# Linear attention and a mixture of four experts: batch 0's attention in head pairs and token halves, and a written order for every engine up to tile 1

## The chip, the core and the metric

The kernel runs on one core of one Trainium2 chip. The time is in device microseconds (us) of that core, the median of several executions. Engines: TensorE (PE: products; PEld: its weight loads), VectorE (DVE), ScalarE (ACT), GpSimd (POOL) and SyncE (SP), and 16 DMA engines. DMAs are asked for by SP, ACT or POOL; POOL's can change the type on the way.

## What is computed

```python
# q, k, v: (8, 8, 576, 64) float32; w1: (4, 512, 1024); w2: (4, 1024, 512); domain_probs: (4608, 4)
def attn(q, k, v):
    phi = lambda x: np.where(x > 0, x, np.exp(x) - 1.0) + 1.0
    q_p, k_p = phi(q), phi(k)
    kv = np.einsum('bhsd,bhse->bhde', k_p, v)
    num = np.einsum('bhsd,bhde->bhse', q_p, kv)
    den = np.einsum('bhsd,bhd->bhs', q_p, k_p.sum(axis=2))[..., None] + 1e-06
    return num / den

x = attn(q, k, v).transpose(0, 2, 1, 3).reshape(4608, 512)
p = domain_probs / (domain_probs.sum(-1, keepdims=True) + 1e-09)
out = sum(p[:, e:e+1] * (np.maximum(x @ w1[e], 0) @ w2[e]) for e in range(4))
```

phi(x) is min(exp(x), max(x + 1, 1)), and that is how the kernel makes it.

## The kernel before

Tokens go in nine tiles of 512. Tile j < 8 is batch j's tokens 0 to 511; tile 8 is the eight leftovers of 64 tokens. All weights stay in SBUF in float16. For a tile, each expert runs layer 1 (512 to 1024, then ReLU) and layer 2 (1024 to 512, added into `acc` with the token's share `p`). Tile 0 runs expert 0's layer 1 plainly (`layer1_group`, L552: eight groups of four 128x512 products) and its layer 2 plainly for all experts (`layer2_part`, L607). Everything else is Strassen-like with seven products for eight: layer 1 in `Block` (`p1` to `p7`, L761), layer 2 in `layer2_product` (L696), with sums of weights on DVE (`weight_sums`, `weight_sums2`), of tokens (`token_sum`) and of hidden rows (`hidden_sum`, POOL, L663 to L669).

Attention of a batch: raw q, k, v arrive in four pieces each of two heads and 512 tokens (four tokens a partition, 1 KB runs), and the 64 leftover tokens apart (`rl`). `phi_act` takes exp on ACT, `phi_dve` the rest on DVE; `vcast` (L339) casts v and leaves room for a column of ones, which gives the denominator; `kv` (L444, and L436 or L452 for the leftovers) makes the 64x65 sums of a pair of heads, and copies its two diagonal blocks into `kvz`, zero elsewhere (L468); `pe_qT` turns q (L423); `nd` (L492) makes numerators and denominators, 128x130 a product; `norm` (L474, L475) takes the reciprocal and multiplies; `pe_xT` (L529, copy L531) turns x so that layer 1 can read it. A leftover x is turned at L414.

Order: every engine runs its instructions in the order in which the program emits them. For batch 0 that order is `CFG["START"]`, a list of steps in which a number n means n filler products (`warm`, L888) on a tile of zeros. All later work is put at positions (`put_at`, from `CFG["ATTN"]`, `L2P`, `BLK` and so on), sorted, and emitted whole: a step's products and the copies behind them come together.

DMA: batch 0's raw tiles are asked for by SP and ACT (L277, L255; `CFG["B0"]`), the weights and batch 1's raw tiles by POOL (`load_first`; L185 for w1 of expert 0 in quarters, L188 for other w1, L182 for w2; order `CFG["DMA"]`), later batches by SP. PSUM has eight banks as four tags of two buffers: `s`, `e`, `b`, `py`; attention's tiles take their tag in turn (`aps`).

Of the kernel before, what the change touches and what calls it, by code (L numbers as in the profile page):

```python
# [1 line left out]

# [18 lines left out]
    "DMA": ('w100', 'w101', 'w102', 'w103', 'k0', 'w201', 'lk1', 'w200', 'w111', 'w110', 'w121', 'w120', 'lv0', 'lk0', 'w211', 'w210', 'v2', 'v1', 'v0', 'k1', 'w130', 'lv1', 'w131', 'q0', 'k2', 'k3', 'v3', 'w220', 'q2', 'q1', 'w221', 'q3', 'w230', 'w231'),  # L21
# [51 lines left out]
    "MODE": {'k0': 0, 'q2': 1, 'k3': 0, 'q0': 0, 'k2': 0, 'k1': 1, 'q1': 0, 'q3': 0, 'T3': 0, 'T0': 0, 'T1': 1, 'v1': 2, 'v2': 0, 'v3': 2, 'v0': 0, 'T2': 1},  # L73
    "APS": ('s', 'e', 'b', 'py'),
    "START": (11, 'qa1', 'qa0', 'ka0', 'qd1', 'lv', 'qd0', 2, 'qT1', 'kd0', 5, 'qT0', 'ka1', 'v1', 'lka', 'lkd', 'v0', 7, 'kv0', 'qa2', 'kd1', 'ka2', 'qa3', 3, 'nd0', 'kd2', 7, 'kv1', 'qd2', 'v2', 'qd3', 'dma0', 'v3', 4, 'nd1', 'qT2', 1, 'kv2', 'ka3', 3, 'xT0', 'dma1', 'kd3', 'qT3', 'nd2', 'xT1', 1, 'kv3', 'ph1', 1, 'nd3', 'ph2', 'xT2', 'xT3', 1, 'ph0'),
    "B0": ('slk', 'aq0', 'slv', 'aq1', 'sv0', 'sv1', 'sq2', 'sk2', 'ak0', 'sq3', 'sv2', 'sv3', 'ak1', 'sk3'),
    "CAST": (),
}
# [3 lines left out]
def kernel(  # L82
# [11 lines left out]
    CAST = CFG["CAST"]  # L94
    ATTN, HSUM, L2ORD, L2AT, MODE = (CFG[x] for x in ("ATTN", "HSUM", "L2ORD", "L2AT", "MODE"))
# [32 lines left out]
    make_identity(nc, identh)  # L128

# [14 lines left out]
    w1_sb = [pw.tile([P, DC, F], FP16, tag=f"w1_{e}", name=f"w1_{e}") for e in range(E)]  # L144
    w2_sb = [pw.tile([P, FC, Dm], FP16, tag=f"w2_{e}", name=f"w2_{e}") for e in range(E)]
# [5 lines left out]
    s1_sb = [pw.tile([P, 3, 2, F // 2], FP16, tag=f"s1_{e}", name=f"s1_{e}") for e in range(E)]  # L151


    t2_sb = {e: pw.tile([P, 3, FH, DH], FP16, tag=f"t2_{e}", name=f"t2_{e}") for e in SE}
# [9 lines left out]
    turn = {"aps": ["s", "e"], "ph": ["b", "py"]}  # L164

    def bank(kind, shape, dtype, name):
        tag = turn[kind][0]
        turn[kind] = turn[kind][1:] + [tag]
        return ppm.tile(shape, dtype, tag=tag, bufs=2, name=name)

    def aps(shape, dtype, name):
        return bank("aps", shape, dtype, name)

# [4 lines left out]
    def load_w(layer, e, r):  # L178

        if layer == 2:  # L180
            fs = slice(r * 4, r * 4 + 4)
            nc.gpsimd.dma_start(out=w2_sb[e][:, fs], in_=w2_src[e, :, fs])  # L182
        elif e == 0:
            fs = slice(r * F // 4, (r + 1) * F // 4)
            nc.gpsimd.dma_start(out=w1_sb[e][:, :, fs], in_=w1_src[e, :, :, fs])  # L185
        else:
            ds = slice(r * 2, r * 2 + 2)
            nc.gpsimd.dma_start(out=w1_sb[e][:, ds], in_=w1_src[e, :, ds])  # L188

    def load_first(lo, hi):  # L190

        parts = [x for x in CFG["DMA"] if x[0] in "kq"]
        homes = dict(zip(parts, [None] * NRAW + ["acc", None]))
        homes.update(v0="hs1", v1="hs1", v2="hs3", v3="hs3")
        if lo > 0:
            b1.alloc_left()
        for x in CFG["DMA"][lo:hi]:
            if x[0] == "w":
                load_w(*map(int, x[1:]))
            elif x[0] == "l":  # L200
                b1.load_left(x[1], eng=nc.gpsimd, us=(int(x[2]),))
            else:
                b1.load(x[0], int(x[1]), nc.gpsimd, home=homes[x])

    def load_probs(eng, first):
# [12 lines left out]
        raws.append(t)  # L218

    def emit_probs(first):  # L220
        t = raws.pop()[:, 0:1] if first else raws.pop()[:, 1:NTILES]
# [14 lines left out]
    raws = []  # L236
# [3 lines left out]
    class Batch:  # L240
        def __init__(self, b):
            self.b = b
            self.raw, self.ph, self.pairs = {}, {}, {}
            self.kvz, self.kl, self.qTl = kvzs[min(b, 1)], kz, qz
            self.ps = b >= 1
# [4 lines left out]
        def load_left(self, *names, eng=nc.sync, us=(0, 1)):  # L250
            b = self.b
            for i, (name, src) in enumerate((("k", k), ("v", v), ("q", q))):
# [9 lines left out]
        def load(self, name, i, eng=nc.sync, home=None):  # L262
# [3 lines left out]
            if home is None:  # L266
                t = praw.tile(shape, FP16 if self.b == 1 and name in CAST else FP32, tag="raw", name="rawb")
# [14 lines left out]
        def alloc(self):  # L282
            self.kp = pa.tile([P, CM, H, D], FP16, tag="kp", bufs=1, name="kp")
            if self.b == 1:
                self.vp = bts[0].vp
            else:
                self.vp = pa.tile([P, CM, H, DE], FP16, tag="vp", bufs=1, name="vp")
                nc.gpsimd.memset(self.vp[:, :, :, D:DE], 1.0 / SX)
            self.vl = vl
            if self.b < 1:  # L290
                self.qp = pm.tile([P, CM, H, D], FP16, tag="h", bufs=NHB, name="qp")
            if self.b < 1:
                self.diag = pa.tile([P, 2, DE], FP16, tag="xsl", bufs=1, name="diag")
                nc.gpsimd.memset(self.diag, 0.0)
                for u in range(2):
                    nc.gpsimd.memset(self.diag[u * HP : (u + 1) * HP, u], 1.0)
            self.qT = pa.tile([P, CM, NPAIR, P], FP16, tag="qT", bufs=1, name="qT")
            if self.b < 1:
                self.x = pm.tile([P, NPAIR, CM, P], FP16, tag="tt", bufs=2, name="x_sb")
            if self.b < 1:  # L300
                self.new_xT()
# [4 lines left out]
        def phi(self, name, i):  # L306
            self.phi_act(name, i)
            self.phi_dve(name, i)

        def phi_act(self, name, i):  # L310

            if self.b >= 1 and (name, i) == ("q", 0):
# [3 lines left out]
            if self.ps or MODE.get(f"{name}{i}") == 1:  # L316
                nc.scalar.activation(dst.rearrange("p c h d -> p h c d"), src, AF.Identity, bias=1.0)
                ee = aps([P, HQ * CM * D], FP32, "psum_ee")
            else:
                ee = pm.tile([P, HQ * CM * D], FP16, tag="hs0", bufs=2, name="ee")  # L320
            ee = ee.rearrange("p (c h d) -> p c h d", c=CM, h=HQ)
            nc.scalar.activation(ee.rearrange("p c h d -> p h c d"), src, AF.Exp)
            self.ph[name, i] = src, dst, ee

        def phi_dve(self, name, i):
            src, dst, ee = self.ph.pop((name, i))
            dst, ee = (a.rearrange("p c h d -> p c (h d)") for a in (dst, ee))
            if self.ps or MODE.get(f"{name}{i}") == 1:
                nc.vector.scalar_tensor_tensor(
                    out=dst, in0=dst, scalar=1.0, in1=ee, op0=AO.max, op1=AO.min  # L330
                )
            else:
                hd = dst.rearrange("p c (h d) -> p h c d", h=HQ)
                (nc.gpsimd if MODE.get(f"{name}{i}") == 2 else nc.vector).tensor_scalar(hd, src, 1.0, 1.0, AO.add, AO.max)
                nc.vector.tensor_tensor(out=dst, in0=ee, in1=dst, op=AO.min)

        def vcast(self, i):
            eng = nc.gpsimd if self.b == 0 and MODE.get(f"v{i}") == 2 else nc.scalar
            (eng.copy if eng is nc.scalar else eng.tensor_copy)(  # L339
# [4 lines left out]
        def left_act(self, *names):  # L344

            for name in names:
# [3 lines left out]
                if name == "k" and self.b < 1:  # L350
                    self.kn = pa.tile([P, HG, D], FP16, tag="qlp", bufs=1, name="kn")
                    parts.append((slice(0, P), self.kn.rearrange("p h d -> p (h d)")))
                for u in range(2) if name == "k" and self.b >= 1 else ():
# [5 lines left out]
                if self.ps:  # L359
                    for us, dst in parts:  # L360
                        nc.scalar.activation(dst, src[us], AF.Identity, bias=1.0)
                    el = aps([P, HG * D], FP32, "psum_el")
                else:
                    el = pm.tile([P, HG * D], FP16, tag="hs0", bufs=2, name="el")
                nc.scalar.activation(el, src, AF.Exp)
                self.ph["l" + name] = src, el, parts

        def left_v(self, eng=nc.scalar):
            (eng.copy if eng is nc.scalar else eng.tensor_copy)(
                out=self.vl[:, :, 0:D], in_=self.rl[:, 1]  # L370
            )

        def left_dve(self, name):
            src, el, parts = self.ph.pop("l" + name)
            for us, dst in parts:
                if self.ps:
                    nc.vector.scalar_tensor_tensor(
                        out=dst, in0=dst, scalar=1.0, in1=el[us], op0=AO.max, op1=AO.min
                    )
                else:  # L380
                    nc.vector.tensor_scalar(dst, src[us], 1.0, 1.0, AO.add, AO.max)
                    nc.vector.tensor_tensor(out=dst, in0=el[us], in1=dst, op=AO.min)

        def left_kv(self):
            self.left_act("k")
            self.left_dve("k")
            self.left_v(nc.gpsimd)

        def dma_qT(self):
# [671 lines left out]
```

## Time and profile before

| | |
|---|---|
| median of 3 runs | 496.31 us (495.79 to 496.56) |
| the profiled execution's span | 494.1 us |
| HBM read, written | 45.16 MB, 9.44 MB |
| DMA, mean over the span | 109 GB/s |
| PE fillers (L888) | 46 products of 128x512 |

The profile's page gives busy time by engine, the span in 40 slices, the DMA queues, the chain that ended last and the costliest groups. The trace behind it can be asked for busy time by stretch, a timeline by engine, and who waited for whom. Products are pipelined and their ends are modelled, so a product's price is better read from the start of one to the start of the next than from its mean duration. POOL's DMA rows give bytes as written (float16); twice as many are read where float32 weights are cast.

### The profile page before, as it was taken

The page shows a single profiled execution, that of the slowest core. Times are in us where ns is not written, and L with a number is a line of the kernel's source. Part 1 is how long each engine was busy: PE and PEld are TensorE (multiplying, and loading weights), DVE is VectorE, ACT ScalarE, POOL GpSimd, SP SyncE. Part 2 cuts the span into 40 slices and gives each one's busy share as a digit, 9 for nine tenths or more (in the row PEclk, how much of TensorE's full clock was granted, in tenths as well). Part 3 has the DMA queues.
Part 4 walks back from the last instruction along what each step waited for, and adds up shares of the span by engine and source line. Part 5 has one row for each costly group of instructions (what it writes and reads, how often), then busy time and mean ns, then how long its engine had stood idle before and what let it go on. Part 6 is the DMA issues. An engine that isn't in the chain of part 4 may idle for free.

```text
span 494.1 us, 11611 instructions
## 1 busy us (share of the span) xinstructions
PE 483.7 (98%) x4346; PEld 409.3 (83%) x4346; DVE 379.5 (77%) x800; ACT 336.7 (68%) x678; POOL 357.0 (72%) x344
## 2 busy tenths in 40 slices
PE   9999999999999999999999999999999999999996
PEld 3557656878898989898989898989898888888885
DVE  5639988799867987698859886888687756775686
ACT  6768969954988488848894789468954565446530
POOL 3735204878977797769776977698669877987775
PEclk9999999999999999999999999999999999999999
DMA  8999966542465234533464255523231020002003
GB/s 261 222 214 247 262 134 189 161 106 49 110 188 116 55 111 161 132 69 93 134 165 82 71 150 139 102 53 94 87 74 35 4 96 1 1 1 87 1 1 86
DMA packets 82104, 53.65 MB, mean 109 GB/s; under 512 B 46240, under 2 KB 75808, under 8 KB 82048
## 3 DMA queue, kind: packets, MB, share of 16 engines
q1 hardware_dynamic: 70512, 40.00, 31.0%
q0 software_dynamic: 9888, 11.41, 12.2%
q10 hardware_dynamic: 1648, 1.51, 1.1%
q8 instruction: 34, 0.56, 0.5%
q14 instruction: 22, 0.18, 0.1%
HBM read 45.16 MB, written 9.44 MB: 111 GB/s over the span
## 4 chain that ended last, share of the span: by engine, by line
PE 79%; DMA 11%; DVE 5%; ACT 3%; POOL 1%; issue 1%; SPq 0%; ACTq 0%; DVEq 0%
PE py L696 37%; PE pb L761 21%; PE pe L761 16%; DMA w<-in_moe_w_dram 9%; DVE acc L598 2%; PE py L607 1%; DMA rawb<-in_v_dram 1%; DVE x_sb L475 1%; PE psum_nd L492 1%; PE psum_kv L444 1%; DVE h L745 1%; POOL w L185 1%; DMA rawh<-in_q_dram 1%; PE pb L696 1%; ACT u L772 0%
## 5 line engine op out<-in xcount | busy, mean ns | idle before, releaser
L598 DVE SCALAR_TENSOR_TENSOR acc<-py,p_sb,acc 128x256 f32<-128x256 f32 (+1 forms) x382 | 182.4, 488 | 44.3 <-PE py L696 39.6
L745 DVE CUSTOM_DVE_ANT_0 h<-pe,u 128x512 f16<-128x512 f32 x140 | 96.4, 688 | 44.1 <-PE pe L761 26.1
L761 PEld LDWEIGHTS <-w 128*128 128x128 f16 x1120 | 108.9, 98 | 17.3 <-issue 1.2
L663 POOL TENSOR_TENSOR hs<-h 128x512 f16<-128x512 f16 x64 | 74.2, 1159 | 54.4 <-DVE h L745 53.3
L696 PEld LDWEIGHTS <-h 128*128 128x128 f16 x1024 | 99.6, 98 | 12.3 <-issue 0.9
L696 PE MATMUL py<-w,h 128*128 128x256 f16 x744 | 106.4, 273 | 0.0
L772 ACT COPY u<-pb 128x512 f32<-128x512 f32 x140 | 83.0, 593 | 27.4 <-PE pb L761 25.5
L665 POOL TENSOR_TENSOR hs<-hs,h 128x512 f16<-128x512 f16 x64 | 74.3, 1160 | 27.5 <-PE py L696 24.9
L761 PEld LDWEIGHTS <-s 128*128 128x128 f16 x840 | 81.6, 98 | 11.9
L761 PE MATMUL pb<-tt,w 128*128 128x256 f16 x560 | 84.0, 273 | 0.1
L696 PEld LDWEIGHTS <-hs 128*128 128x128 f16 x768 | 74.4, 98 | 8.8 <-issue 0.4
L669 POOL TENSOR_TENSOR hs<-h,hs 128x512 f16<-128x512 f16 x64 | 75.3, 1177 | 3.6 <-PE py L696 3.2
L696 PE MATMUL py<-t,hs 128*128 128x256 f16 x496 | 74.4, 273 | 0.1
L667 POOL TENSOR_TENSOR h<-h 128x512 f16<-128x512 f16 x64 | 74.3, 1162 | 0.0
L787 ACT ACTIVATE h<-pe 128x512 f16<-128x512 f32 x70 | 42.0, 600 | 45.0 <-PE pe L761 44.2
L781 ACT COPY pe<-pb 128x512 f32<-128x512 f32 x70 | 40.1, 573 | 41.6 <-PE pb L761 15.4
L805 ACT ACTIVATE h<-pb 128x512 f16<-128x512 f32 x70 | 42.1, 601 | 9.6 <-PE pb L761 9.5
L761 PE MATMUL pe<-tt,s 128*128 128x256 f16 x280 | 42.0, 273 | 0.0
L761 PE MATMUL pb<-tt,s 128*128 128x256 f16 x280 | 42.0, 273 | 0.0
L761 PE MATMUL pb<-xT,w 128*128 128x256 f16 x248 | 37.2, 273 | 0.4 <-DMA w<-in_moe_w_dram 0.4
L761 PE MATMUL pe<-xT,w 128*128 128x256 f16 x248 | 37.2, 273 | 0.3 <-ACT pe L781 0.3
L761 PE MATMUL pe<-xT,s 128*128 128x256 f16 x248 | 37.2, 273 | 0.0
(125 smaller groups left out, 609.6 us busy)
## 6 DMA issues: line engine op xcount, KB each, us to landing
out_dram<-acc SPq DMA_DIRECT2D x32, 256.0 KB, 2.5
w<-in_moe_w_dram POOLq DMA_DIRECT2D x14, 512.0 KB, 12.2
rawb<-in_v_dram SPq DMA_DIRECT2D x26, 256.0 KB, 2.8
rawb<-in_q_dram SPq DMA_DIRECT2D x26, 256.0 KB, 2.8
rawb<-in_k_dram SPq DMA_DIRECT2D x26, 256.0 KB, 3.2
w<-in_moe_w_dram POOLq DMA_DIRECT2D x4, 256.0 KB, 5.7
rawb<-in_k_dram POOLq DMA_DIRECT2D x4, 256.0 KB, 8.0
rl<-in_q_dram SPq DMA_DIRECT2D x16, 64.0 KB, 2.7
```

What stands on the lines that cost most here:

```text
L598: nc.vector.scalar_tensor_tensor(out=acc, in0=ps, scalar=pscal, in1=acc, op0=AO.mult, op1=AO.add)
L663: nc.gpsimd.tensor_tensor(out=hs[0], in0=a21, in1=a22, op=AO.add)
L665: nc.gpsimd.tensor_tensor(out=hs[1], in0=hs[0], in1=a11, op=AO.subtract)
L667: nc.gpsimd.tensor_tensor(out=a21, in0=a11, in1=a21, op=AO.subtract)
L669: nc.gpsimd.tensor_tensor(out=hs[3], in0=a12, in1=hs[1], op=AO.subtract)
L696: nc.tensor.matmul(out=ps, lhsT=lhsT(k), rhs=rhs[:, k], start=first and k == 0, stop=k == FH - 1, skip_group_check=True,)
L745: nc.vector._custom_dve(TENSOR_ADD_SAT, out=out, in0=ps, in1=u, s0=BIG, s1=0.0)
L761: nc.tensor.matmul(out=ps[:, kk], lhsT=lk(kc), rhs=rhs[:, kc], start=first and kk == 0 and kc == 0, stop=kc == 1, skip_group_check=True,)
L772: nc.scalar.copy(u, self.b)
L781: nc.scalar.copy(self.e5, self.b)
L787: nc.scalar.activation(self.h[:, :, 0, 0:NH], self.e5, AF.Relu)
L805: nc.scalar.activation(self.h[:, :, 1, 0:NH], self.b, AF.Relu)
```

## The change

Batch 0 gets a class of its own (`First`). Its k and v come as pairs of heads, all 576 tokens, nine tokens a partition (64 partitions a head), so that batch 0 has no leftover k and v apart. Its q comes in four pieces: a half of the tokens (two of four a partition) of four heads. The sums of k and v are 18 products of 64x65 for a pair, one head into PSUM partitions 0 to 63 and the other into 64 to 127. q and x are turned by halves of the tokens; numerators of two pairs go into one PSUM tile and their denominators into another, with one reciprocal and one multiplication for both. Layer 1 of expert 0 in tile 0 runs by halves of the tokens, two groups of 128 hidden rows together (`layer1_half`). Tiles for raw k and v and their results use the space of weights that come later (`s1`, `t2`, `w1`, `w2` of experts 2 and 3). ACT no longer asks for DMAs at the start. Batches 1 to 7 keep their attention, but batch 1's numerators are emitted in two halves, and phi has one form (`phi_act`, `phi_dve` with exp in PSUM).

Most functions become generators: a `yield` parts the products from the copies behind them. `CFG["EARLY"]` names, in order, which function goes on next, from the first load up to tile 2's first blocks; it replaces `START`, `B0`, `MODE` and `APS`. Names: `lq`, `lk`, `lv` loads; `ke`, `kl`, `km` exp, add-and-max, min of k; `qe`, `ql`, `qm` the same of q; `vc` cast of v; `qT`, `xT` transposes; `nd` numerators; `Lgh` layer 1 of row group g and half h; `p1.010` product 1 of tile 0, expert 1, half 0; `y0.12` layer 2 of expert 0, rows 1, part 2; `s`, `t` weight sums; `m` layer 2 products; `b1.` batch 1. What is left after the list is emitted in the order before. `CFG["BANK"]` names the PSUM tag of a step.

```diff
+    "CUT": (((0, 3, 4), (0, 3, 4), (0, 4), (0, 4)), ((0, 2, 4),) * 4),
+    "WARM": (14, 5, 3, 1, 2, 1, 1),
-    "START": (11, 'qa1', 'qa0', 'ka0', 'qd1', 'lv', 'qd0', 2, 'qT1', 'kd0', 5, 'qT0', 'ka1', 'v1', 'lka', 'lkd', 'v0', 7, 'kv0', 'qa2', 'kd1', 'ka2', 'qa3', 3, 'nd0', 'kd2', 7, 'kv1', 'qd2', 'v2', 'qd3', 'dma0', 'v3', 4, 'nd1', 'qT2', 1, 'kv2', 'ka3', 3, 'xT0', 'dma1', 'kd3', 'qT3', 'nd2', 'xT1', 1, 'kv3', 'ph1', 1, 'nd3', 'ph2', 'xT2', 'xT3', 1, 'ph0'),
-    "B0": ('slk', 'aq0', 'slv', 'aq1', 'sv0', 'sv1', 'sq2', 'sk2', 'ak0', 'sq3', 'sv2', 'sv3', 'ak1', 'sk3'),
+    "EARLY": (
+        "lq0 lk3 lk1 ql0 qe0 lq2 ke1 ql2 kl1 w103 qe2 ke3 kl3 lv1 w100 lk0 lq1 km1 qm0 ke0 kl0 w102 w101 km3 warm0 qT0 ql1 lv0 qm2 km0 vc1 vc0 w111 lq3 ql3 qT0",
+        "warm1 kv1 kv1 lk2 qe3 lv2 vc2 kv1 qT2 qT2 lv3 rk1 kv0 w110 ke2 qe1 kv0 kv0 qm3 vc3 kl2 warm2 nd01 nd00 warm3 qT3 v0 nd00 w200 nd01 warm4 xT10 kv3 xT11",
+        "km2 kv2 kv2 qT3 xT11 xT10 kv2 xT01 kv3 w201 kv3 qm1 xT01 warm5 qT1 rk0 xT00 nd11 qT1 xT00 L01 rv1 nd10 nd11 warm6 xT31 nd10 rv0 L21 w120 xT21 L11 xT31",
+        "L31 xT21 L31 lpr0 L01 L31 xT20 xT20 k3 xT30 L11 w121 L01 v2 xT30 s0.0 L21 v1 L30 L11 L30 L20 L10 L21 p1.010 ts0.0 L20 p1.010 L00 ts0.2 b1.v0 L10 ts0.1",
...
+        "s2.0 s2.1 s2.3 b1.v1 p2.021 y0.13 p2.020 p6.020 p6.021 p6.020 t0.3 s2.2 y0.23 p6.021 b1.km3 p5.020 p7.020 b1.v2 q2 y0.23 s0.2 y1.10 t1.0 p7.020",
+        "c22.020 b1.k1 p5.021 y1.11 p7.021 p7.021 w131 b1.km1 b1.k0 p4.020 p3.020 y1.20 y1.21 q0 b1.k2 p4.020 p4.021 c22.021 p3.020 b1.load5 p3.021 b1.km0",
+        "y1.12 b1.v3 p4.021 b1.kv0 b1.km2 b1.load0 b1.kv0 y1.13 b1.kv1 b1.kv1 p3.021 y1.22 y1.23 b1.q3 y1.30 y1.13 y1.23 q1 y1.31 y1.32 y1.33 b1.q2 p1.031",
...
+    kraw = [pw.tile([P, 2, TK, D], FP32, tag=f"{x}_{E - 1}", name=f"kraw{x}") for x in ("s1", "t2")]
+    vraw = [pw.tile([P, 2, TK, D], FP32, tag=f"{x}_{E - 2}", name=f"vraw{x}") for x in ("s1", "t2")]
+    kpos = pw.tile([P, NPAIR, TK, D], FP16, tag=f"w1_{E - 1}", name="kpos")
+    kexp = pw.tile([P, NPAIR, TK, D], FP16, tag=f"w2_{E - 1}", name="kexp")
+    vpos = pw.tile([P, NPAIR, TK, DE], FP16, tag=f"w2_{E - 2}", name="vpos")
...
+    class First(Batch):
...
+        def load_kv(self, name, i, eng):
+            t, src = {"k": (kraw, k), "v": (vraw, v)}[name]
+            eng.dma_start(
+                out=t[i // 2][:, i % 2].rearrange("p t d -> p (t d)"),
+                in_=src[0, 2 * i : 2 * i + 2].rearrange("h (p t) d -> (h p) (t d)", t=TK),
+            )
...
+        def q_lin(self, i, eng):
+            eng.tensor_scalar(self.q_part(i), self.raw["q", i], 1.0, 1.0, AO.add, AO.max)
...
+        def kv(self, i, engs):
+            ps = aps([P, DE], FP32, "psum_kv")
+            for t in range(TK):
+                for u in range(2):
+                    us = slice(u * HP, (u + 1) * HP)
+                    nc.tensor.matmul(
+                        out=ps[us],
+                        lhsT=kpos[us, i, t],
+                        rhs=vpos[us, i, t],
+                        start=t == 0,
+                        stop=t == TK - 1,
+                        skip_group_check=True,
+                    )
+            for u in range(2):
+                yield
+                us = slice(u * HP, (u + 1) * HP)
+                (engs[u].copy if engs[u] is nc.scalar else engs[u].tensor_copy)(
+                    out=self.kvz[us, i, u], in_=ps[us]
+                )
+
+        def x_norm(self, g, hf):
+            num = aps([P, 2, 2, 2, D], FP32, "psum_num")
+            den = aps([P, 2, 2, 2], FP32, "psum_den", "+")
+            for a in range(2):
+                for c in range(2):
+                    pair, lhsT = 2 * g + a, self.qT[:, 2 * hf + c, 2 * g + a]
+                    for ps, cols in ((num[:, a, c], slice(0, D)), (den[:, a, c], slice(D, DE))):
+                        nc.tensor.matmul(out=ps, lhsT=lhsT, rhs=self.kvz[:, pair, :, cols], start=True, stop=True)
+            yield
+            recip = pa.tile([P, 2, 2, 2, 1], FP32, tag="recip", bufs=3, name="recip")
+            nc.vector.reciprocal(recip, den)
+            nc.vector.tensor_tensor(
+                out=self.x[:, 2 * g : 2 * g + 2, 2 * hf : 2 * hf + 2].rearrange("p a c (u d) -> p a c u d", u=2),
+                in0=num,
+                in1=recip.broadcast_to([P, 2, 2, 2, D]),
+                op=AO.mult,
+            )
...
+    def layer1_half(g, hf, hT, cuts):
+        ps = aps([P, 2, NH], FP32, "ph")
+        for lo, hi in zip(cuts, cuts[1:]):
+            for kk in range(2):
+                fj = 2 * g + kk
+                for dc in range(lo, hi):
+                    nc.tensor.matmul(
+                        out=ps[:, kk],
+                        lhsT=w1_sb[0][:, dc, fj * P : (fj + 1) * P],
+                        rhs=b0.xT[:, dc, hf * NH : (hf + 1) * NH],
+                        start=kk == 0 and dc == 0,
+                        stop=dc == DC - 1,
+                        skip_group_check=True,
+                    )
+            yield
+        nc.scalar.activation(hT[g % 2][:, :, g // 2, hf * NH : (hf + 1) * NH], ps, AF.Relu)
...
+        for name in " ".join(CFG["EARLY"]).split():
+            advance(name)
+        for name in [w[2] for w in work]:
+            while name in live:
+                advance(name)
```

## The prediction

> **What bounds the kernel now.** I read the page's busy shares and chain first, then busy time by stretch, then TensorE's timeline where a stretch falls short, then the DMA queues.
>
> ```profile
> PE 483.7 (98%) x4346; PEld 409.3 (83%) x4346; DVE 379.5 (77%) x800; ACT 336.7 (68%) x678; POOL 357.0 (72%) x344
> ...
> PE 79%; DMA 11%; DVE 5%; ACT 3%; POOL 1%; issue 1%; SPq 0%; ACTq 0%; DVEq 0%
> ```
>
> TensorE sets the end: its products in order are the time, and only gaps or work that isn't needed can go. By stretch (busy time and number for PE, PEld, DVE, ACT, POOL; clock; DMA share; GB/s):
>
> ```profile
> 0.00:20.00 20.00, 18.55 (x119) 9.37 (x120) 13.40 (x39) 12.93 (x28) 11.47 (x26) 1.00 1.07 248
> 20.00:60.00 40.00, 39.25 (x270) 25.24 (x269) 27.97 (x50) 32.45 (x64) 15.91 (x23) 1.00 1.18 239
> 60.00:72.00 12.00, 10.35 (x83) 6.12 (x84) 10.07 (x26) 7.39 (x15) 0.00 (x0) 1.00 0.86 169
> 72.00:104.00 32.00, 31.65 (x265) 24.40 (x264) 26.79 (x45) 30.93 (x69) 21.79 (x19) 1.00 0.56 159
> 104.00:108.00 4.00, 2.89 (x28) 2.28 (x26) 3.90 (x7) 1.63 (x4) 3.26 (x3) 1.00 0.47 103
> ...
> 140.00:480.00 340.00, 339.98 (x3207) 305.59 (x3206) 259.49 (x552) 229.33 (x458) 270.06 (x243) 1.00 0.32 81
> ```
>
> From 140 us on nothing is idle, and the new order list ends before that; so the change can only win or lose ahead of 140. Before 20 us PE looks busy, but its timeline shows with what:
>
> ```profile
> 1.19 5.58 PE L888 MATMUL warm_ps<-qz 128*128 128x512 f16 x13 [1.19 <-DVE qz L134]
> ...
> 19.96 6.21 PE L552 MATMUL ph<-xT,w 128*128 128x512 f16 x28
> ...
> 30.50 0.61 PE L761 MATMUL pb<-xT,w 128*128 128x256 f16 x4 [0.44 <-DMA w<-in_moe_w_dram]
> ...
> 60.83 1.45 PE L607 MATMUL py<-w,h 128*128 128x512 f16 x6 [0.47 <-DMA w<-in_moe_w_dram]
> ...
> 68.00 0.29 PE L492 MATMUL psum_nd<-kvz,qT 128*128 128x130 f16 x2 [0.26 <-DVE x_sb L475]
> ...
> 106.07 0.34 PE L492 MATMUL psum_nd<-kvz,qT 128*128 128x130 f16 x3 [0.50 <-DMA qT<-qp]
> 107.02 0.27 PE L414 MATMUL psum_xl<-identh,x_sl 128*128 128x128 f16 x2 [0.60 <-DVE qlp L377]
> ```
>
> Fillers (46 in all) keep it going; useful products run without a break from 19.96. Rows give the price of a product when nothing waits, by starts: 128x256 0.109 us (four from 34.42 to 34.86), 128x512 0.215, 128x130 or a transpose 0.055. Taking the start of each product to the start of the next, less this price, I count 7.0 us lost from 20 to 140: 1.05 at 30 to 32 (a weight, then a copy), 0.6 at 60.8 (a weight), 2.3 from 65.8 to 71.3 (batch 1's numerators wait for the norm before them, 0.43 each, four times, and smaller ones), 1.4 at 105 to 107, and 1.6 in seven pieces of 0.13 to 0.36 (37 to 117). The DMA engines are full from 3 to 69 us, so this stretch has a second floor:
>
> ```profile
> q10 hardware_dynamic: 956, 0.92, 75.2%
> q1 hardware_dynamic: 1025, 0.27, 30.2%
> ...
> q0 software_dynamic: 1753, 0.87, 143.5%
> ...
> q0 software_dynamic: 710, 0.94, 73.2%
> q1 hardware_dynamic: 704, 0.69, 40.6%
> ```
>
> The first pair is 2.5 to 6.5 us (packets, MB, share of 16 engines), the third 13.5 to 18, the last pair 54 to 60. Share times stretch times 16 over packets is a packet's time: 50 ns for the 1 KB of q10, 19 ns for the 256 B of q1, and 41 ns between starts for expert 0's weight quarters. The last pair shows that two busy queues take turns packet by packet (710 to 704).
>
> **Part 1, batch 0's loads.** Twelve pieces of 256 packets of 1 KB and four leftovers of 256 packets of 256 B cost 12 x 0.80 + 4 x 0.30 = 10.8 us of all engines. Now q comes as four pieces of 512 packets of 512 B, k and v as eight of 128 packets of 2304 B. No row has these sizes; on the line through 19 and 50 ns they are 29 and 103 ns: 4 x 0.94 + 8 x 0.82 = 10.3 us. Bounds: 512 B as dear as 1 KB gives 13.0, and all at the 348 GB/s of the stretch 8 to 12 gives 9.8. I take 10.3, the line, 0.5 less than before.
> [...]
>
> **Part 2, the race with the weights.** POOL issued w1_0 at 10.16 us, after a cast of v, and its packets ran from about 12.5, as the raw loads ran out (the last, issued by SP at 8.37, landed 5.6 later, 13.97). In the new order POOL issues w1_0 after one add-and-max of q (0.67 to 1.16, the casts of L339 and the sums of L663), whose load is the fourth: landing at 5.7, issue near 6.5, packets near 8.8. Then about 2.5 us of raw loads are left, which take turns with weight packets: 103 against 41 ns, so two thirds of the engines, and the last v lands near 13.3 (11.9 alone; 17 to 18.6 if the weights take the 64% of the last pair above). w1_0 ends near 17.8 instead of 19.2.
>
> **Part 3, the chain to layer 1.** From the last v: cast 0.65 (L339 row), 18 kv products 0.5 to 1.0 (0.027 by columns, 0.055 as a 130-wide pair of load and product; I take 0.045), copies of 64x65 0.45, numerators 0.45, reciprocal 0.2, the joint norm of 512 columns 0.6 to 0.7 (half as wide takes 0.42 at L475), transposes and copy 0.6. DVE is the tighter string: after the q piece of 10.5 us it has add-and-max 0.4, three copies, min, add-and-max, two joint norms (0.8 each with reciprocal), min, copies and min, which puts the second norm's end at 18.0. Products of layer 1 then run without a break from about 18.2, with one quarter group (4 x 0.109) done before; before, 19.96 with 4 x 0.215 done. What is left at that point is 60 x 0.109 and 8 transposes, 7.0, against 28 x 0.215 = 6.0. Gain 1.76 - 0.96 = 0.8 us. The filler products fall from 46 to 27; both lie before this point and cost nothing; nor do the 72 small kv products (1.1 us before, 2 to 4 now), whose cover is the wait for loads. Bounds -4.5 (last v at 18.6) to +2.5.
> [...] Here the first 12 fillers start 0.427 apart and those from 6.3 us on 0.215. [...]
>
> **Part 4, the order to tile 1.** Expert 1's Strassen blocks now start before layer 2 of expert 0; weights of expert 1 come before those of layer 2. Counting w at 2.45 us (512 KB written at 209 KB/us) and raw pieces at 0.75 to 0.9 in POOL's new order, each weight lands ahead of its first product but one: w2_1's second half now stands behind five raw loads, lands at 45 to 46, and PE would be there at 44.2: 1.0 us lost; w2_2's second half lands near 62, when it is needed. All that PE has queued waits behind that product, expert 2's blocks first. Against it, of the 3.3 us of the two old weight waits and the small pieces I count 1.3 back, less than half, since ACT and DVE (10.00 of 10 us of DVE in 50 to 60) end many of them. Batch 1's numerators are now pairs with other products between: of 2.3 us I count 1.7 back. The transpose of the leftover x moves behind tile 1's expert 1 (0.6 of the 107 us wait), and batch 2's q transposes are asked for earlier: 1.2 of 1.4. ACT is 31 of 32 us busy from 72 to 104, which is why I don't take more there. Sum 1.3 - 1.0 + 1.7 + 1.2 = 3.2; bounds -2 (nothing regained, the weight wait doubled) to +6.5 (all but half a microsecond, no weight wait).
>
> **Sum.** 0.8 + 3.2 = 4.0 us off the profiled span of 494.1: 490.1. The median stands 2.2 above that span, so 492.3.
>
> **Rivals.** *The raw loads lose the race.* If weight packets take 64% from 8.8 us, the last v lands at 18.6, layer 1 runs from 23.5, and POOL, whose next weights queue behind its own cast of v (waiting for a load of the same race), issues them late too, which eats the 0.3 net of the weight terms: 0.8 - 5.3 + 2.9 = -1.6, 497.9. For: POOL asks for weights 3.6 us earlier than before. Against: k and v packets are 2.3 KB, twice a weight's. It decides from a last v after about 17.3.
> *The weights take it back.* DMA is full to 69 us; if w2_1 and w2_2 halves come 2 to 3 us late, PE's lead is waited away: 495.5 to 496.7, no change. For: bytes to move are the same. Against: before, only 1.7 us of waits name a weight.
> [...]
> That the change doesn't do what it says: the instruction order shows all named parts in place, so no chance is kept for it.
>
> **Numbers.** Forecast (489.5 to 494.5) 0.62; nearly all 0.12; weights take it back 0.12; lost race 0.14. A measurement here tells 0.2% (1 us) from no change. Faster: 0.62 + 0.12 + 0.02 of the third case = 0.76; same 0.08; slower 0.14 + 0.02 = 0.16. The range leaves out the worst of the lost race and the best of the fourth: 487.5 to 497.8.
>
> **What would show it.** Right: the continuous run of layer 1 starts at 17 to 19 us; last v landed by 14.5; no stretch of PE spacing at 0.43 us after 8 us; TensorE waiting about 1 us for a weight near 45; gaps below 3.5 us in all from 20 to 140. Wrong: layer 1 later than 20, products at half clock in it, or weight waits above 3 us together. From 140 on the stretches must be the same.

## The result, and the profile after

The changed kernel took 491.94 us in the median of 4 runs (491.75 to 493.09), the kernel before 496.44 beside it (495.79 to 496.67): a ratio of 0.9921, with a 95% interval of 0.9907 to 0.9936. Timed again later, with another set of runs, it took 492.45 (492.16 to 492.92), ratio 0.9918 (0.9905 to 0.9930). The forecast was 492.3. The profiled span is 490.2, where the sum had given 490.1. So the total was right; its two terms were not, as will be seen.

Busy shares and the chain, from the page of the kernel after:

```profile
PE 478.1 (98%) x4427; PEld 410.9 (84%) x4427; DVE 382.4 (78%) x801; ACT 332.9 (68%) x670; POOL 358.8 (73%) x341
...
PE 91%; DVE 4%; ACT 1%; DMA 1%; issue 1%; SPq 1%; DVEq 0%; ACTq 0%
```

PE is busy 5.6 us less, most of it before 20 us (18.55 to 13.97), where 19 fillers are gone (4.1 at 0.215 each). No useful product was saved: there are 100 more of them, and their columns add up to 0.9 us more. In the chain the share of DMA went from 11% to 1%: the run of loads and weights that led it is now a run of products. Busy time by stretch of the kernel after (PE, PEld, DVE, ACT, POOL with the number of instructions; clock; DMA share; GB/s):

```profile
0.00:20.00 20.00, 13.97 (x163) 7.64 (x164) 13.80 (x36) 10.08 (x19) 12.09 (x22) 1.00 1.03 244
20.00:60.00 40.00, 39.88 (x315) 28.74 (x314) 29.90 (x58) 34.62 (x70) 15.66 (x22) 1.00 1.18 242
60.00:72.00 12.00, 12.00 (x105) 8.55 (x103) 11.03 (x21) 10.45 (x24) 5.55 (x6) 1.00 0.75 131
72.00:104.00 32.00, 30.71 (x258) 23.54 (x257) 30.33 (x54) 25.54 (x55) 16.79 (x13) 1.00 0.70 180
104.00:108.00 4.00, 4.00 (x42) 3.63 (x40) 3.76 (x9) 2.47 (x5) 4.00 (x5) 1.00 0.20 37
...
140.00:480.00 340.00, 339.70 (x3199) 305.18 (x3198) 259.87 (x554) 226.72 (x452) 271.56 (x244) 1.00 0.30 80
```

Against the same rows of before, 60 to 72 went from 10.35 to 12.00 and 104 to 108 from 2.89 to 4.00; 72 to 104 lost 0.9; from 140 on PE's row is the same to 0.3 us. Taking product starts less the price of a product, the pauses of 0.12 us and more from 20 to 140 are 2.1 us, where they were 7.0 (with all smaller ones some 3.3 and 7.5).

Busy time can't tell how far a kernel has got. For that I added up, from the trace, the columns of all products that start after a given time, fillers left out, at 2.4 columns a nanosecond (the rows give 512 columns in 0.215 us): the useful product time still to run, in us.

| kernel | at 20 | at 60 | at 72 | at 100 | at 140 | span |
|---|---|---|---|---|---|---|
| before | 450.6 | 413.0 | 404.0 | 377.6 | 340.2 | 494.1 |
| after | 451.3 | 412.8 | 401.2 | 375.7 | 336.8 | 490.2 |
| after, timed again | 451.1 | 412.4 | 400.7 | 375.3 | 336.4 | 490.5 |
| e4_old_order | 451.5 | 414.0 | 404.9 | 378.1 | 340.6 | 494.7 |
| e6_nd_row | 451.0 | 412.7 | 405.2 | 379.9 | 341.1 | 494.7 |
| e3_no_fill | 452.1 | 414.5 | 402.9 | 377.4 | 338.4 | 491.9 |
| e1_w_first | 454.8 | 423.9 | 412.3 | 386.2 | 347.8 | 501.7 |
| e2_norm_late | 450.3 | 412.7 | 401.1 | 375.8 | 336.9 | 490.5 |
| e5_t2_later | 451.6 | 413.0 | 401.4 | 375.1 | 336.2 | 490.1 |

At 20 us the changed kernel is 0.7 us *behind* the kernel before. From 20 to 140 it gains 0.9 (to 60), 2.6 (to 72), gives 0.9 back (to 100) and gains 1.5 (to 140): 4.1 in all (0.5 behind and 4.3 in its second profile). The other 0.5 us of the 3.9 came behind 140 us, where the span less the product time left varies from one execution to the next (13.9 before, 13.4 after, 14.1 in the second profile); so that part can't be put down to the change. The start, the largest part of the diff, earned nothing.

What the start looks like, on PE's timeline of the kernel after (start, time, engine, line, operation; in brackets the idle time before and what ended it):

```profile
1.19 4.64 PE L1003 MATMUL warm_ps<-qz 128*128 128x512 f16 x14 [1.19 <-DVE qz L175]
8.26 0.40 PE L601 MATMUL psum_qT<-identh,qp 128*128 128x128 f16 x4 [2.43 <-DVE qp L593]
...
17.84 0.40 PE L601 MATMUL psum_qT<-identh,qp 128*128 128x128 f16 x4 [1.02 <-DVE qp L593]
...
19.81 0.60 PE L661 MATMUL ph<-xT,w 128*128 128x256 f16 x4
```

From the last of these rows on layer 1 runs without a break (18.2 in the prediction). Both pauses wait for a minimum of q on DVE. On POOL:

```profile
7.14 2.35 POOL L590 TENSOR_SCALAR qp<-rawq 128x512 f16<-128x512 f32 x1 [5.71 <-DMA rawq<-in_q_dram]
9.45 3.26 POOL L226 DMA_DIRECT2D w<-in_moe_w_dram  x4
```

The load that the add-and-max needs landed at 7.06 (5.7 predicted), and it took 2.35 us (I had 0.67 to 1.16), so w1_0 was asked for at 9.45 instead of 6.5 and landed in quarters from 14.54 to 20.39. The last v had landed at 12.94: the race between weights and raw loads hardly took place.

### The profile page after: what moved, and what is told of

Its sections match the earlier page's. It is cut to its first block, busy times and chain, and to the rows that moved or that the text cites. A ratio compares the mean times of both kernels' runs of the same rounds, so it can differ in the third digit from the quotient of the medians.

```text
span 490.2 us, 11736 instructions
## 1 busy us (share of the span) xinstructions
PE 478.1 (98%) x4427; PEld 410.9 (84%) x4427; DVE 382.4 (78%) x801; ACT 332.9 (68%) x670; POOL 358.8 (73%) x341
## 4 chain that ended last, share of the span: by engine, by line
PE 91%; DVE 4%; ACT 1%; DMA 1%; issue 1%; SPq 1%; DVEq 0%; ACTq 0%
PE py L816 39%; PE pb L873 24%; PE pe L873 18%; PE py L721 4%; PE ph L661 1%; PE psum_nd L478 1%; DMA rawq<-in_q_dram 1%; PE psum_kv L442 1%; DVE acc L712 1%; PE pb L816 1%; SPq L546 0%; PE psum_nl L496 0%; PE pe L816 0%; DVE t L768 0%; DVE x_sb L638 0%
## 5 line engine op out<-in xcount | busy, mean ns | idle before, releaser
L899 ACT COPY pe<-pb 128x512 f32<-128x512 f32 x70 | 40.2, 576 | 39.3 <-PE pb L873 13.9
```

The lines of the kernel that those rows point to most:

```text
L899: nc.scalar.copy(self.e5, self.b)
```

## The experiments

Edits of the written order are shown by their steps. `w100` to `w103` are the quarters of expert 0's w1; `s` and `t` steps are weight sums; numbers after a label are medians of 4 to 11 runs, with the ratio to the kernel before, timed beside them.

### e4_old_order: the new start, then the old order

```diff
...
- L20 L10 L21 p1.010 ts0.0 L20 p1.010 L00 ts0.2 b1.v0 L10 ts0.1
...
+ L20 L10 L21 L20 L00 L10 L10 L00 L00 k0 w201 rk1 w200 w111 w110 w121
...
```

The list ends after layer 1 of expert 0, followed by weights and batch 1's loads in the order of `CFG["DMA"]`; all that came later in it is put at positions again.

> The changed kernel's own start (batch 0's loads, sums, norms, layer 1 by halves) up to its last layer 1 group, then the weights in the old order on POOL and everything else at the old positions. Theory A (the gain of 3.9 us lies in the order from 20 to 140 us, and the new start alone is 0.7 us behind the old one at 20 us): near the kernel before or a little over it, 495.5 to 498, with the old gaps back at 30 to 32, 65 to 71 and 105 to 107. Rival B (the layout of batch 0's loads and its halves bring the gain, the order only follows): 491 to 493.5. In between, 493.5 to 495.5, both share it.

Measured 497.29, ratio 1.0015 (1.0003 to 1.0028): the whole gain is gone. The old pauses are back (1.6 us by starts at 26 to 34, 1.4 at 106 to 108), and so is the row of numerators. Busy time from 60 to 72, then PE's timeline there:

```profile
60.00:72.00 12.00, 10.70 (x88) 6.46 (x86) 10.26 (x26) 7.79 (x15) 0.00 (x0) 1.00 0.83 171
```

```profile
68.29 0.29 PE L452 MATMUL psum_nd<-kvz,qT 128*128 128x130 f16 x2 [0.26 <-DVE x_sb L440]
68.83 0.29 PE L452 MATMUL psum_nd<-kvz,qT 128*128 128x130 f16 x2 [0.26 <-DVE x_sb L440]
69.39 0.29 PE L452 MATMUL psum_nd<-kvz,qT 128*128 128x130 f16 x2 [0.26 <-DVE x_sb L440]
```

So the order is the gain, and the start by itself costs some 0.7 us, as the table has it at 20 us. From 20 to 72 the order is worth 3.5 us against this kernel (414.0 - 404.9 = 9.1 of 12 us used, 11.6 in the changed one; 1.0 to 60).

### e6_nd_row: batch 1's numerators in a row again

```diff
...
- b1.qT3 b1.nd30 y1.03 s3.3 b1.qT2 b1.nd21 b1.loadlq p6.030
...
- b1.nd01 b1.qT1 p3.030 b1.xT2 b1.nd00 b1.nd10 b1.nd01 y2.20 b1.xT3 b1.nd11 y2.21
...
+ b1.qT1 b1.nd30 b1.nd30 b1.nd31 b1.nd31 b1.nd20 b1.nd20 b1.nd21 b1.nd21 b1.nd00 b1.nd00
+ b1.nd01 b1.nd01 b1.nd10 b1.nd10 b1.nd11 b1.nd11 b1.xT3 b1.xT3 b1.xT2 b1.xT2
...
```

> The changed kernel with batch 1's eight numerator groups put together again, each followed at once by its normalization, as the kernel before had them; all else as in the changed kernel. Theory A (of the order's gain some 1.4 to 1.7 us is that these groups lie spread between expert products, so that no product waits for VectorE's normalization): waits of 0.4 us between the numerator groups come back at 65 to 73 us, and the time is 493.0 to 493.8. Rival: the gain there came from the shift of work that feeds the groups (copies, minimums), and the row costs nothing; 491.7 to 492.4.

Measured 496.43, ratio 1.0000 (0.9988 to 1.0011), 4.0 us above the changed kernel of the same set, twice what theory A said. The table puts nearly all of it at 60 to 72 (412.7 to 405.2, 7.5 us done instead of 11.6). The edit also puts batch 1's transposes of x right behind the row. Its rows by stretch and from PE's timeline:

```profile
60.00:64.00 4.00, 2.53 (x26) 1.63 (x23) 2.91 (x11) 1.45 (x3) 0.00 (x0) 1.00 1.11 150
64.00:68.00 4.00, 3.48 (x26) 2.89 (x27) 1.88 (x8) 2.60 (x6) 0.61 (x2) 0.57 0.00 0
```

```profile
62.57 0.84 PE L478 MATMUL psum_nd<-kvz,qT 128*128 128x130 f16 x6 [0.26 <-DVE x_sb L466]
64.22 0.54 PE L478 MATMUL psum_nd<-kvz,qT 128*128 128x130 f16 x4 [0.81 <-DVE x_sb L466]
66.34 0.58 PE L518 MATMUL psum_xT<-identh,x_sb 128*128 128x128 f16 x4 [0.31 <-ACT xT L522]
```

Six waits make 3.1 us by starts, and in this execution the granted clock also fell: 0.57 in the mean from 64 to 68 us. Two of its executions have a mean clock of 1.000 and still took 495.95 and 496.38, 3.5 to 3.9 above the changed kernel: the place of these steps costs that much without a fall of the clock. What a fall adds is not settled. The row is a harder one than before's, which had layer 2 products between its pieces.

### e5_t2_later: a weight sum moved behind POOL's sums

The wait that the change brought (1.05 us by starts):

```profile
75.95 0.60 PE L873 MATMUL pb<-tt,w 128*128 128x256 f16 x4 [0.89 <-ACT u L884]
```

Behind ACT's `u` stands a longer story, on DVE and on POOL of the kernel after:

```profile
68.58 3.42 DVE L768 TENSOR_TENSOR t<-w 128x1024 f16<-128x1024 f16 x1
```

```profile
67.27 1.15 POOL L854 TENSOR_TENSOR tt<-xT,tt 128x512 f16<-128x512 f16 x1
68.37 0.78 POOL L223 DMA_DIRECT2D w<-in_moe_w_dram  x1
69.17 1.17 POOL L854 TENSOR_TENSOR tt<-xT,tt 128x512 f16<-128x512 f16 x1
70.29 1.16 POOL L854 TENSOR_TENSOR tt<-xT 128x512 f16<-128x512 f16 x1
```

```diff
...
- y2.33 b1.load3 t2.0 b2.lv p2.101 p6.100 p6.100 y2.33 b2.lkm y2.10 y2.11 t2.1
+ y2.33 b1.load3 b2.lv p2.101 p6.100 p6.100 y2.33 b2.lkm y2.10 y2.11 t2.0 t2.1
...
```

> One sum of layer 2 weights of expert 2 on VectorE goes two steps of its queue later (behind a scaled add and batch 2's leftover k). In the changed kernel it takes 3.42 us instead of 0.69, while POOL runs four token sums of 1.16 us, and ScalarE and then TensorE (1.05 us at 74.8) wait behind it. Theory A (the sum is held off as long as POOL's sums run): started later it is shorter, the wait of TensorE at 74.8 goes, time 490.7 to 491.5. Rival B (the wait comes from something else, or moves on): 491.7 to 492.4.

Measured 491.83 (491.69 to 492.52), ratio 0.9906 (0.9891 to 0.9921). DVE's row of this kernel:

```profile
72.11 0.69 DVE L768 TENSOR_TENSOR t<-w 128x1024 f16<-128x1024 f16 x1
```

The same sum takes 0.69 us once POOL's sums have ended, and the wait of 1.05 is gone (0.26 for a weight, which landed at 76.03, came in its place). By the table it does 0.8 us more from 60 to 100 (37.9 against 37.1); its median is 0.1 to 0.6 below the changed kernel's two, inside their intervals. That the sum is short once POOL's sums have ended is shown, the gain in time is not.

### e3_no_fill: no filler products at all

```diff
-    "WARM": (14, 5, 3, 1, 2, 1, 1),
+    "WARM": (),
```

> The changed kernel without its 27 filler products; nothing else differs. Theory A (they keep TensorE's clock up): products of batch 0 and the first of layer 1 are spaced at half speed (0.21 to 0.22 us for 256 columns), the clock rises some 3 to 5 us after layer 1 begins, and 1.7 to 2.5 us are lost: 493.5 to 494.5. Rival B (the small products of batch 0 keep it up by themselves, fillers cost and give nothing): 491.5 to 492.3, spacing 0.109 from the first group of layer 1 on.

Measured 494.08 (493.66 to 494.68), ratio 0.9949 (0.9935 to 0.9964): 2.1 us above the changed kernel. PE's timeline:

```profile
9.82 0.70 PE L612 MATMUL psum_kv<-vpos,kpos 64*64 64x65 f16 x18 [1.06 <-ACT vpos L579]
...
19.68 1.01 PE L661 MATMUL ph<-xT,w 128*128 128x256 f16 x4
```

With fillers the same 18 products take 0.48 and the same four 0.60. By starts the four from 19.68 take 0.81 here, against 0.44 from 18.52 in the kernel after, and the 18 take 0.64 against 0.41; the four from 21.23 still take 0.83, and the 16 from 22.18 are at full pace (1.91). (The clock column shows 1.00 for this stretch too, so the spacing is the measure here.)

### e1_w_first: the weights asked for before anything else

```diff
- lq0 lk3 lk1 ql0 qe0 lq2 ke1 ql2 kl1 w103 qe2 ke3 kl3 lv1 w100 lk0 lq1 km1 qm0 ke0 kl0 w102 w101
+ w103 w100 w102 w101 lq0 lk3 lk1 ql0 qe0 lq2 ke1 ql2 kl1 qe2 ke3 kl3 lv1 lk0 lq1 km1 qm0 ke0 kl0
...
```

> POOL asks for w1 of expert 0 first of all, at about 1.3 us, ahead of its add-and-max of q, which holds it to 9.45 us in the changed kernel. The race of the prediction at its sharpest. Theory A (packets take turns, raw loads are on the path of batch 0): the last v lands at 15 to 18 instead of 12.9, layer 1 runs without a break from 22 to 24 instead of 19.7, and the time is 493 to 496. Rival B (weights were the late ones: their last quarter lands at 20.4, after the break-free run has begun): the run starts at 20 or before and the time is 490 to 492.

Measured 503.94, ratio 1.0144 (1.0113 to 1.0175). POOL asks for w1_0 at 1.38, the last v lands at 22.82, and PE waits and then runs slowly:

```profile
13.42 0.48 PE L612 MATMUL psum_kv<-vpos,kpos 64*64 64x65 f16 x18 [2.79 <-ACT vpos L579]
...
21.82 0.29 PE L634 MATMUL psum_num<-kvz,qT 128*128 128x128 f16 x1 [3.26 <-ACT qT L603]
```

```profile
16.00:30.00 14.00, 9.60 (x106) 6.20 (x106) 6.55 (x20) 4.86 (x12) 7.80 (x12) 0.50 0.86 176
```

This is the lost race of the prediction's first rival, brought about by the order. It is dearer than expected, and the clock fell with it: 0.50 in the mean of the 14 us above. How the 12 us part between race and clock wasn't tried.

### e2_norm_late and e7_both: another order for DVE's start

```diff
...
- vc3 kl2 warm2 nd01 nd00 warm3 qT3 v0 nd00 w200 nd01 warm4 xT10 kv3 xT11 km2 kv2 kv2 qT3
...
+ vc3 kl2 warm2 nd01 warm3 qT3 v0 km2 nd01 qT3 w200 kv2 kv3 kv2 kv2 kv3 kv3 warm4 xT01 xT11
+ xT01 xT11 w201 nd11 L31 L01 nd11 nd00 L21 xT31 xT21 xT31 xT21 nd00 rk0 qm1 L31
...
```

> Start of the changed kernel in another order for VectorE: the minimum of the last k tile (km2) goes ahead of the joint norms of half 0, half 1 of the tokens is normalized before the second pair of half 0, q's part 1 is turned last, and layer 1 begins with group 3. Nothing else changes; the two last fillers go. Theory D (VectorE's queue is what ends the start: in the changed kernel it runs back to back from 10.8 us and km2 stands behind two joint norms at 15.41 us): the unbroken run of layer 1 begins at 17.5 to 18.5 us in place of 19.69, and the time is 490.3 to 491.5. Rival W (the first weights end the start: in the changed kernel w1_0's pieces landed 14.54 to 20.39 us, and the next expert's w1 follows them): layer 1 starts sooner but waits for weights, or layer 1 begins no sooner; time 491.7 to 493.

> The order of the start of e2_norm_late and the later token sum of e5_t2_later together. If the two gains add: 490.0 to 491.2, below the changed kernel by 0.7 to 1.9 us. If weights end the start: as e5_t2_later, 491.4 to 492.2.

e2_norm_late took 493.84 (492.25 to 494.2), ratio 0.9936 (0.9922 to 0.9950), its profiled span 490.5. e7_both took 491.55 (491.47 to 493.28), ratio 0.9911 (0.9896 to 0.9926). Layer 1 begins at 16.19 in the first, and then stops again and again; PE's timeline has between the pieces:

```profile
18.68 0.60 PE L661 MATMUL ph<-xT,w 128*128 128x256 f16 x4 [0.46 <-ACT xT L650]
```

At 24 us the product time left is 447.0, the changed kernel's 447.5 and 447.2: both theories fall. No weight is waited for, and no run begins at 18; the waits are for copies and norms. e2_norm_late is 0.3 us longer than the changed kernel by its profiled span, but 1.4 to 1.9 by its median. The granted clock parts its executions: the two with a mean of 0.998 took 492.3 and 492.4, the four with 0.994 to 0.997 took 493.8 to 494.2 (e7_both: 491.5 with 0.998 to 1.000, 493.0 and 493.3 with 0.995). The profile of e7_both shows such a fall. PE's timeline, then the busy times by stretch, whose 0.50 is the granted clock:

```profile
8.43 0.61 PE L601 MATMUL psum_qT<-identh,qp 128*128 128x128 f16 x4 [2.16 <-DVE qp L593]
8.83 2.34 PE L1003 MATMUL warm_ps<-qz 128*128 128x512 f16 x5
```

```profile
9.00:11.00 2.00, 2.00 (x6) 0.45 (x3) 1.75 (x5) 1.57 (x3) 2.00 (x3) 0.50 1.08 384
```

After a pause of 2.16 us the clock fell to half here, and the five fillers took 2.34 us (1.24 in the kernel after, whose pause was 2.43 and whose clock stayed).

### e9_cover and e10_late_cover: the pause filled

```diff
-    "WARM": (14, 5, 3, 1, 2, 1, 1),
+    "WARM": (18, 5, 3, 1, 2, 1, 1),
```

> The changed kernel with 18 fillers ahead of the first turn of q in place of 14, nothing else. Theory C (TensorE's pause of 2.2 to 2.4 us between the 14th filler and the first turn can cost the clock: in the profile of e7_both, whose pause ran from 6.27 to 8.43 us, the granted clock was 0.50 from about 8.7 to 11.6 us, while the changed kernel's profile, pause 5.85 to 8.26, shows no fall; so part of the timed runs lose over a microsecond there): with the pause cut by four products (0.21 us each) the clock stays and the time is 490.8 to 491.8, its runs closer together. Rival (the pause costs nothing in the timed runs, and fillers that run late push the first turn back): 492.0 to 493.0.

> e7_both (order of the start of e2_norm_late, later token sum) with 18 fillers first in place of 14. If the clock that fell at the pause is why e2_norm_late measured 493.84 with a profiled span no longer than the changed kernel's: 490.5 to 491.5. If VectorE's amount of work bounds the start whatever its order, and the clock does not matter: 491.4 to 492.4.

e9_cover took 492.71 (492.41 to 494.43), ratio 0.9930 (0.9917 to 0.9943); e10_late_cover 492.47 (491.11 to 493.54), ratio 0.9927 (0.9912 to 0.9942). Theory C falls as a remedy, and e9_cover's time lies in the rival's range; e10_late_cover's lies in neither of its two. Four of e9_cover's five executions have a mean clock of 1.000 and took 492.4 to 492.8, no less than the changed kernel; in the fifth, 494.43, the clock fell at the *second* pause (0.50 from 19 to 22 us). In e10_late_cover the two executions with a mean clock of 0.994 took 493.3 and 493.5, the other four 491.1 to 492.5: the clock still fell in some, filled pause or not. So the executions whose clock fell took 0.8 to 2.4 us longer here, and four more fillers did not keep the fall away.

### e11_act and e12_qm1: what the second pause waits for

```diff
-    "QT": 'VVAV',
+    "QT": 'VVAA',
...
-    "XT": ('AA', 'VV', 'VA', 'VV'),
+    "XT": ('AA', 'AA', 'VA', 'VV'),
```

It also has 18 fillers first and e5_t2_later's edit.

> The changed kernel with 18 fillers first, the token sum later as in e5_t2_later, and three copies of the start (of q's turn in part 3, and of x's turn in both halves of pair 1) given from VectorE to ScalarE, which is idle for 2 us at 14.4 to 16.4 us. Theory V (VectorE's amount of work from 10.8 to 20.5 us, not its order, sets the start: the new order of e2_norm_late brought its first layer-1 product forward to 16.19 us and gave it all back in five waits by 22 us): some 0.9 us less on VectorE there, the unbroken run of layer 1 begins at 18.6 to 19.2 us, and the time is 490.0 to 491.2. Rival: the chain moves to ScalarE's copies or to the k and v loads, layer 1 begins at 19.4 to 20.2 and the time stays at 491.3 to 492.2.

Measured 493.97 (492.91 to 494.6), ratio 0.9956 (0.9944 to 0.9968): slower than the changed kernel, and than e9_cover, though DVE has less to do. Part of it is the clock: five of its six executions have a mean of 0.994 to 0.996 and took 493.8 to 494.6; the profiled one, with 1.000, took 492.91. DVE's rows of the kernel after, and then of e11_act:

```profile
15.41 0.45 DVE L576 TENSOR_TENSOR kpos<-kexp,kpos 128x576 f16<-128x576 f16 x1
...
17.12 0.23 DVE L623 CAST kvz<-psum_kv 64x65 f16<-64x65 f32 x1 [0.53 <-ACT kvz L623]
17.36 0.43 DVE L593 TENSOR_TENSOR qp<-ee,qp 128x512 f16<-128x512 f16 x1
...
18.94 0.69 DVE L638 TENSOR_TENSOR x_sb<-psum_num,recip 128x512 f16<-128x512 f32 x1
```

```profile
15.83 0.45 DVE L576 TENSOR_TENSOR kpos<-kexp,kpos 128x576 f16<-128x576 f16 x1
18.56 0.23 DVE L623 CAST kvz<-psum_kv 64x65 f16<-64x65 f32 x1 [2.29 <-ACT kvz L623]
18.80 0.42 DVE L593 TENSOR_TENSOR qp<-ee,qp 128x512 f16<-128x512 f16 x1
```

The minimum of q's part 1 needs nothing of the cast that it stands behind; but the cast waits for ACT, and ACT now has three copies ahead of the last two of its own casts. So it is a place in a queue that holds the minimum up. e12_qm1 moves it (with e5_t2_later's edit, 14 fillers):

```diff
...
- km2 kv2 kv2 qT3 xT11 xT10 kv2 xT01 kv3 w201 kv3 qm1 xT01 warm5 qT1 rk0 xT00 nd11 qT1 xT00
+ km2 qm1 kv2 kv2 qT3 xT11 xT10 qT1 kv2 xT01 kv3 w201 kv3 xT01 warm5 qT1 rk0 xT00 nd11 xT00
...
```

> e5_t2_later with one more move in the start: the minimum of q's part 1 (qm1) goes ahead of the casts of batch 0's k-v products on VectorE, and its turn to just after the first transposes of x. Theory Q (what ends the start is a place in VectorE's queue: in the changed kernel qm1, ready since about 15 us, stood behind a cast that waited for ScalarE until 17.12, began at 17.36, and TensorE waited 1.18 us for it; in e11_act, where ScalarE had three copies more ahead of that cast, the cast began at 18.56 and qm1 at 18.80): qm1 begins at 15.8 to 16.4 us, the pause of TensorE at 16.2 to 17.6 shrinks below 0.4 us, the unbroken run of layer 1 begins at 18.4 to 19.2 in place of 19.69, and the time is 490.7 to 491.5. Rival (the work that is left on VectorE and ScalarE, or the first weights, ends the start all the same): layer 1's run at 19.4 to 20 us, 491.5 to 492.3.

Measured 491.55 (491.26 to 492.11), ratio 0.9908 (0.9895 to 0.9922). DVE's and PE's rows:

```profile
16.65 0.45 DVE L576 TENSOR_TENSOR kpos<-kexp,kpos 128x576 f16<-128x576 f16 x1
17.02 0.42 DVE L593 TENSOR_TENSOR qp<-ee,qp 128x512 f16<-128x512 f16 x1
...
18.36 0.23 DVE L623 CAST kvz<-psum_kv 64x65 f16<-64x65 f32 x1 [0.20 <-ACT kvz L623]
```

```profile
18.15 0.38 PE L601 MATMUL psum_qT<-identh,qp 128*128 128x128 f16 x4 [0.52 <-ACT kvz L623]
...
20.44 0.60 PE L661 MATMUL ph<-xT,w 128*128 128x256 f16 x4
```

The whole start of this execution lies 1.2 us later (its k piece `lk1` landed at 6.84, not 6.24, and the clock fell behind its first pause, to 0.50 from 9 to 12 us), so it is read from km2: to the run of layer 1 it is 20.44 - 16.65 = 3.8 us, before 19.81 - 15.41 = 4.4. The pause ahead of the turn went from 1.18 to 0.68 by starts, not below 0.4: now the turn's PSUM tile waits for ACT's casts. In the time, the miss and the hit can't be told apart: 491.55 is within the spread of e5_t2_later.

No version is shown to beat the changed kernel: e5_t2_later, e7_both and e12_qm1 lie 0.1 to 0.9 us below it by medians, and all their intervals overlap.

## Why the prediction was right

The total was right because terms were off in opposite ways, and that is luck: against the forecast the start lost 1.5 us more, the order gained 0.9 more, 0.5 came behind 140 us, and the median stands 1.7 above the profiled span where I had 2.2 (each execution's time is 1.7 to 1.9 above its own span; I had set the median beside the span of one faster execution).

**The bound.** Right: PE's products in order are the time, the gain lies between 20 and 140 us, and from 140 on the rows differ by 0.3 us (339.70 against 339.98), less than two executions of one kernel do.

**Part 1, loads.** Right: in the mean the packets took 27 ns (512 B; 29 predicted) and 103 ns (2304 B; 103). A piece of q came to 0.87 us, where the line gave 0.94. The last v landed at 12.94 (13.3).

**Part 2, the race.** The order of events was as told, two steps mis-sized: the fourth load landed 1.4 us later, and the add-and-max took 2.35 us, so the issue came 3 us later than I put it and the quarters landed up to 20.39 (17.8). The bound of 17 to 18.6 for the last v doesn't come out of its own terms either: 2.5 us of loads at 36% of the engines are 6.9 us, which gives some 16.3. The late weights cost nothing, since layer 1 was late too; and e1_w_first shows that the rival was real: with the weights at the front it costs 12 us.

**Part 3, the start: +0.8 predicted, -0.7 measured** (at 20 us; by its ratio e4_old_order, which has the start alone, is 0.7 us above the kernel before, 0.1 to 1.4). The step that failed is "DVE is the tighter string ... puts the second norm's end at 18.0", the norm from which layer 1's unbroken run was to start. It ended at 19.63 (18.94 + 0.69), and the run with its transposes began at 19.69: 19.96 - 19.69 - 0.96 gives the -0.7. I laid DVE's instructions end to end and let none of them wait. Behind the q piece of 10.7 the trace has a cast that waits 0.53 us for ACT, a copy of a turn that waits 0.49 for PE, an add-and-max of 0.71 where I had 0.4, and a minimum of 0.87 where the others take 0.41 to 0.43: some 1.8 us together, against the 1.6 by which the norm was late. (Another minimum, at 7.38, took 0.83 beside POOL's add-and-max. What lengthened the one of 0.87 is not shown: it ran beside POOL's DMA issues, but so did the one of 0.41 at 9.69.) e11_act and e12_qm1 show the queue place; in e2_norm_late another order of the chain moved the waits and did not shorten their sum. Two smaller terms: a kv product costs 0.023 us by starts, not 0.045; and "fillers cost nothing" is only half the truth: they are worth 2.1 us (e3_no_fill: the first four products of layer 1 take 0.81 us by starts without them, 0.44 with them). The sum charges nothing for a fall of the clock behind a pause. The trace has a pause of 2.43 us, and the clock stayed at 1.00 there, but at the same place it fell to 0.50 in the profiles of e7_both and e12_qm1.

**Part 4, the order: +3.2 predicted, about +4.1 measured.** By pieces: from 20 to 60 us 0.9 came, and 0.6 more with the weight wait at 60.8, where I had 1.3 - 1.0 = 0.3. The weight wait of 1.0 near 45 never came: w2_1's second half landed at 46.30 (45 to 46 predicted), but PE, put there at 44.2, reached the product at 46.43, without a wait. Of these 2.2 us the late start is 1.6, so part of what the start lost was paid back here, which I did not foresee. From 60 to 72 the gain is 2.6; without the weight wait some 2.0 are left for batch 1's numerators, 1.7 predicted. e6_nd_row says the same place can cost 4.0. Behind it a wait that I didn't name took 1.05 back (DVE's weight sum beside POOL's sums). The pieces at 105 to 107: 1.5 measured at 100 to 140, 1.2 predicted.

**Rivals.** *The weights take it back*: no wait for a weight of over 0.15 us is left from 20 to 140, so it fell (of the 1.7 us that I counted for weights before, 0.44 waited for a copy). *Nearly all*, to which I gave 0.12: in the order it came closer than I thought (2.1 of the 7.0 us of pauses are left), but the start gave nothing, so it failed. The signs named beforehand read: last v by 14.5 right, gaps below 3.5 right, no half speed after 8 us right in this execution, layer 1 at 17 to 19 wrong, weight wait near 45 wrong.

## What to carry to other kernels

A row of small products, each of which waits for a normalization on another engine, is best broken up with products that are ready; in e6_nd_row it cost 4.0 us where its waits add up to 3.1, so test it by putting the row back. When a start is worked out by hand, walk all engines' queues together: an instruction that is ready but stands behind a copy that waits for a third engine is what a sum over one engine leaves out. And compare kernels by the useful work still to run at a time, since fillers keep busy time high whatever has been done.

## What the runs showed of the hardware

One DVE sum of 128x1024 in float16 took 3.42 us beside POOL's sums and 0.69 without them (e5_t2_later), a factor of 5. It began during a DMA issue of POOL, 0.59 us ahead of the next POOL sum, and ended 0.55 us after the second one. Not every DVE instruction was longer there: a scaled add into `acc` of 128x512 took 0.74 inside a POOL sum (66.41, the kernel after) and 0.74 after the last (71.93). What sets the one apart from the other is not shown, nor whether POOL's own 2.35 us for its add-and-max have a like cause.

The granted clock fell to 0.50 after a pause of PE of 2.16 us (e7_both) and of 2.34 (e12_qm1), and in the waits of e6_nd_row, the longest of which is 0.81. It stayed at 1.00 after 2.21 (e2_norm_late), 2.43 (the kernel after) and 3.32 (e1_w_first, 5.83 to 9.15). Ahead of e9_cover's fall PE was idle for 0.80 us of the two from 16 to 18. So the length of the pause does not tell here whether the clock falls, and no experiment shows what does. Four of the falls ahead of a kernel's end lasted 3.41 us (e6_nd_row 64.34 to 67.75, e7_both 8.45 to 11.86, e9_cover 18.64 to 22.05, e12_qm1 8.99 to 12.40), and e1_w_first's 17.07 (14.39 to 31.46), five times as long.

The moment at which the first 14 fillers turn fast, from 0.427 us to 0.215 by starts, is not the same in every execution: they took 4.64 us in the kernel after (fast from 4.15 us on), 5.08 in e7_both and 5.58 in the second profile of the kernel after. So the fillers end sooner or later, and the pause behind them was 2.43, 2.16 and 1.24 us. What moves the moment is not shown.

The landing of the same third load (`lk1`, issued at 1.79 in the kernel after) ranged from 5.57 to 6.84 us in the runs of the new start, apart from e1_w_first's 7.54. In the kernel after it was 6.24, and the last v landed at 12.94. What moves the loads is open.
